# Another order of the same operations, and the buffers that follow from it, in a linear-attention and MoE kernel

## The chip, the core and the metric

One Trainium2 chip, one core. The metric is the time of one launch in device microseconds (us): the median of three runs, with the lowest and highest beside it.

## The reference

Eight batches of eight heads, 576 tokens each, head width 64. A feature map is applied to q and k, a linear attention follows, and its output, as 4608 tokens of width 512, goes through a block with an inner width of 1024. All in float32.

```python
def phi(x):
    proj = np.einsum('bhsd,df->bhsf', x, w_phi)            # 128 features
    proj = proj - np.max(np.abs(proj), axis=-1, keepdims=True)
    return np.concatenate([np.exp(proj), np.exp(-proj)], axis=-1)
q_p, k_p = (phi(q), phi(k))
kv = np.einsum('bhsf,bhsd->bhfd', k_p, v)
z = np.sum(k_p, axis=2)
num = np.einsum('bhsf,bhfd->bhsd', q_p, kv)
den = np.einsum('bhsf,bhf->bhs', q_p, z)[..., None] + 1e-06
# x = num / den, heads side by side: 4608 x 512
h = x @ w_in
sm = softmax(h)
solu = h * sm
ln = (solu - mean(solu)) / np.sqrt(var(solu) + 1e-06) * g_ln
out = ln @ w_out
```

## The kernel before

**Units and tiles.** The attention is cut into 16 units, two to a batch. A unit has two halves, each a pair of heads; the text writes "unit 5, half 1". The second part has 36 tiles of 128 tokens, nine to a pair of batches. One engine queue works on both at once: matmuls of the tiles stand between those of the units.

**One half of a unit.** Keys come in by `k_load` (rawk) and values by `v_load` and `v_half_load` (rawv, vz). TensorE (PE) projects the keys (pjk); VectorE (DVE) takes the largest absolute value of each row (m) and subtracts it (dk); ScalarE (ACT) makes the two exponentials (ek); GpSimd (POOL) sums them over tokens (zt, zacc). Then `visit` does three things without a break on PE: the numerators of the half before (num), the sum of keys times values of this half (kvT), and the denominators of the half before (den). The numerators read kvf, which is kvT turned by way of DRAM: DVE turns blocks (kvs), SyncE (SP) writes them out (dk), and four transfers read them back (kvf). So each visit needs the four reads that follow the visit before. Units 0 to 2 are handled apart: their query features are projected and turned on PE (pjq, dq, dT, fq); units 0 and 1 turn kvT on PE (kvt). Later units use q as loaded twice (rawq), split in two fp32r parts on POOL (hq), projected (pq) and turned on DVE (blk). The denominators are inverted on DVE (dE, cmr), written to DRAM (d) and read back spread over 64 partitions by two transfers (rb); POOL then multiplies (`divide`, xa and xb).

**One tile.** `moe_hi` and `moe_lo` split the input in two fp32r parts (mxh, mxl), `moe_h` multiplies with w_in in two halves of 12 matmuls (h), DVE takes the maximum (nm), ACT the exponential (eu), DVE the product, DVE turns blocks (ub), SP writes them (du) and four transfers read them back (uTs), ACT and POOL split them (uhs, uls), and `moe_o` multiplies with w_out in two halves of 12 matmuls (o). ACT scales the result (os) and SP stores it (out). The last three tiles turn on PE instead (uh, ul).

**Weights.** w_in and w_out arrive as 64-bit floats in eight transfers of 1024 KB (`w_load`, wraw; parts 0 to 3 are w_in, parts 4 to 7 w_out) and are rebuilt as float32: one pass on ACT and three on DVE for each part (`w_rebias`, `w_bits`), then the w_in parts are split (win_h on ACT, win_l on POOL), and the w_out parts are scaled, centred on DVE (`w_center`, eight passes w<-w,cms) and split (w_out_h, w_out_l). The first tile's h needs all four win_l and the division of both units of batch 0.

**What sets the order.** Each operation is registered with `op`, with the operations that it follows and the buffers that it takes. `Plan.order` (line 232) then walks through a table of 2621 operation numbers, `SEQUENCE` (line 50): it checks that what an operation follows stands ahead of it, and gives each new tile the buffer of its kind that was freed first.

```python
        for i in SEQUENCE:
            o = self.ops[i]
            assert written.issuperset(o["after"]), o["name"]
            written.add(o["name"])
            for tag, t in o["alloc"]:
                slot[t] = free[tag].pop(0)
```

`InOrder` (line 255) keeps every instruction in program order. So each engine, and SP's queue of transfers, runs its operations in the order of the table, and an instruction that waits holds up all that stand behind it on its engine. All 595 transfers are issued by SP. All work is recorded in a helper, so nearly every row of the profile has line 263.

Of the kernel before, what the change touches and what calls it, by code (L numbers as in the profile page):

```python
# [50 lines left out]
    88, 99, 0, 3, 2, 136, 126, 132, 102, 7, 89, 90, 100, 103, 198, 104, 199, 127, 107, 95, 108, 91, 101, 96,  # L51
    130, 8, 131, 14, 92, 133, 230, 105, 128, 97, 186, 137, 197, 134, 93, 129, 35, 98, 145, 224, 135, 94, 142,
    138, 106, 148, 9, 109, 149, 143, 139, 144, 118, 140, 234, 146, 150, 41, 10, 15, 187, 114, 11, 141, 151, 119,
    110, 164, 147, 165, 16, 120, 188, 121, 115, 153, 111, 152, 200, 205, 17, 112, 53, 231, 166, 154, 116, 201,
    36, 193, 232, 189, 156, 4, 233, 117, 167, 202, 155, 194, 169, 113, 37, 203, 225, 18, 158, 168, 157, 122,
    204, 190, 195, 28, 295, 38, 196, 6, 42, 226, 39, 12, 191, 228, 13, 170, 192, 235, 227, 171, 229, 172, 240,
    123, 159, 173, 241, 243, 236, 160, 216, 245, 47, 43, 54, 238, 44, 244, 174, 242, 175, 161, 55, 29, 296, 45,
    162, 246, 217, 328, 124, 30, 247, 249, 284, 248, 207, 56, 251, 250, 125, 218, 40, 208, 176, 31, 219, 48,
    209, 32, 177, 178, 179, 210, 49, 163, 252, 180, 212, 46, 237, 213, 254, 50, 214, 253, 255, 215, 51, 211,
    329, 256, 239, 436, 297, 206, 21, 386, 52, 303, 332, 304, 271, 57, 397, 262, 268, 285, 263, 59, 286, 269,  # L60
    333, 60, 58, 220, 633, 437, 330, 291, 273, 61, 264, 287, 270, 22, 331, 292, 272, 298, 221, 257, 438, 293,
    62, 299, 258, 288, 294, 387, 300, 289, 181, 344, 63, 265, 5, 182, 222, 23, 301, 305, 290, 259, 67, 302, 260,
    76, 314, 338, 79, 183, 73, 334, 184, 85, 64, 261, 306, 315, 310, 316, 398, 307, 311, 24, 317, 223, 267, 345,
    266, 346, 68, 19, 33, 65, 274, 20, 308, 275, 276, 309, 34, 335, 278, 277, 347, 279, 439, 349, 339, 348, 336,
    280, 312, 440, 318, 337, 388, 185, 313, 340, 319, 25, 350, 320, 321, 66, 351, 281, 74, 282, 389, 26, 341,
    352, 390, 75, 393, 391, 353, 27, 394, 441, 355, 442, 354, 372, 342, 373, 356, 77, 322, 374, 283, 70, 323,
    468, 358, 366, 1871, 357, 82, 367, 359, 324, 368, 343, 445, 360, 375, 1913, 1872, 443, 69, 395, 1873, 444,
    86, 361, 80, 1914, 446, 362, 377, 447, 550, 469, 614, 81, 405, 392, 1874, 399, 376, 406, 87, 396, 325, 83,
    326, 470, 363, 400, 1875, 448, 327, 369, 401, 511, 1876, 449, 416, 402, 407, 370, 1877, 371, 471, 408, 78,
    1915, 412, 450, 413, 417, 409, 472, 1880, 451, 477, 452, 473, 403, 475, 84, 404, 1916, 474, 410, 1881, 476,  # L70
    501, 551, 418, 478, 479, 453, 422, 1917, 1882, 500, 1883, 378, 552, 853, 1918, 1884, 1885, 379, 512, 1919,
    1892, 364, 411, 71, 1893, 419, 480, 380, 1894, 1886, 1922, 1923, 481, 423, 454, 424, 414, 482, 457, 455, 72,
    381, 458, 555, 553, 483, 1887, 1924, 425, 1895, 554, 484, 459, 1878, 1925, 415, 426, 456, 427, 556, 428,
    1920, 420, 559, 1926, 557, 1888, 1927, 558, 1896, 421, 560, 1897, 365, 429, 1928, 1898, 485, 460, 1901, 461,
    1934, 561, 1929, 486, 582, 1902, 583, 430, 1935, 502, 1903, 462, 382, 463, 520, 1930, 489, 584, 431, 503,
    664, 1904, 507, 519, 504, 505, 1921, 514, 432, 562, 506, 1936, 513, 563, 508, 490, 383, 564, 515, 509, 530,
    433, 516, 491, 1905, 517, 434, 565, 585, 435, 566, 587, 487, 567, 586, 1937, 464, 588, 488, 384, 510, 1906,
    518, 531, 568, 589, 1938, 591, 1931, 696, 590, 532, 1939, 571, 592, 665, 1879, 1940, 536, 572, 385, 1943,
    1932, 593, 1944, 666, 492, 573, 493, 1907, 1945, 1908, 1946, 521, 1947, 494, 697, 1948, 465, 594, 1889, 595,
    569, 615, 522, 596, 570, 698, 526, 523, 537, 524, 667, 538, 525, 597, 1909, 668, 626, 1949, 495, 1933, 533,  # L80
    975, 527, 1890, 625, 528, 466, 529, 496, 1950, 699, 539, 598, 671, 700, 1910, 540, 541, 542, 534, 497, 669,
    627, 673, 670, 498, 1951, 672, 535, 674, 1899, 467, 675, 543, 499, 1941, 574, 1955, 1956, 2018, 599, 1957,
    576, 575, 600, 603, 544, 676, 545, 1958, 677, 577, 778, 678, 2019, 546, 679, 740, 616, 1959, 680, 729, 681,
    547, 628, 617, 1960, 548, 1952, 618, 549, 604, 1961, 619, 620, 621, 601, 644, 622, 2020, 629, 623, 630, 624,
    1964, 1976, 645, 602, 1965, 703, 605, 701, 578, 705, 631, 2021, 810, 682, 632, 646, 702, 704, 706, 1900,
    650, 2022, 1942, 685, 2023, 779, 2024, 606, 683, 2027, 1966, 1967, 1968, 579, 1969, 580, 728, 607, 707,
# [1182 lines left out]
```

## Time and profile before

| what | value |
|---|---|
| median of 3 runs | 719.25 us (719.08 to 719.99) |
| the profiled execution | 717.91 us |
| its span, first to last instruction | 716.1 us |
| granted TensorE clock, mean | 0.997 |
| PE busy | 694.4 us (97%) |
| DVE, ACT, POOL busy | 483.5 (68%), 368.7 (51%), 513.7 us (72%) |
| moved by DMA | 109.96 MB, mean 154 GB/s |

The profiled execution is 1.34 us shorter than the median of the timed runs; 1.8 us of it lie outside the span. A row of the timeline gives the start and the length in us, the engine, the operation, the tiles that are written and read, the shapes and the count, and in brackets the idle time before it with what ended that. Rows of neighbouring like operations are merged. SPq is SP issuing a transfer, not the transfer itself.

### The profile page before, as it was taken

To read this page: it belongs to the slowest core of one execution; us is meant where nothing else is said; L and a number is where in the kernel's file an instruction comes from. 1 tells how busy PE (TensorE), PEld (TensorE's weight loads), DVE (VectorE), ACT (ScalarE), POOL (GpSimd) and SP (SyncE) were. 2 spreads that over 40 slices of the span, in tenths; PEclk is the share of its full clock that TensorE was granted. 3 is DMA by queue.
4 is the path that set the end of the run, shared out by engine and by line. 5 is a ranking of instruction groups with operands and counts; after the bars stand their busy time and mean duration, and the time that the engine had idled before them with its cause. 6 is when DMAs were issued, how large, how long until landed. Compare 5 with 4: busy or idle time off the path is not lost.

```text
span 716.1 us, 13369 instructions
## 1 busy us (share of the span) xinstructions
PE 694.4 (97%) x4858; PEld 517.8 (72%) x4858; DVE 483.5 (68%) x795; ACT 368.7 (51%) x683; POOL 513.7 (72%) x501
## 2 busy tenths in 40 slices
PE   6999889999999999999999999999999999999997
PEld 5656567777777777777776777777787777788886
DVE  5999878656867678478566688676687574544422
ACT  4888645644753555546555555545544554324221
POOL 1136999996889878887978987986877777445151
PEclk9999999999999999999999999999999999999999
DMA  7784365644763565637357367745664443512331
GB/s 258 286 274 103 79 181 167 189 136 118 199 189 121 159 194 159 199 106 205 111 161 183 118 179 185 192 133 139 177 182 119 144 135 77 155 56 72 125 102 75
DMA packets 113649, 109.96 MB, mean 154 GB/s; under 512 B 57648, under 2 KB 90928, under 8 KB 113072
## 3 DMA queue, kind: packets, MB, share of 16 engines
q1 hardware_dynamic: 113584, 109.11, 52.7%
q8 instruction: 39, 0.64, 0.4%
q14 instruction: 26, 0.21, 0.1%
HBM read 76.68 MB, written 32.39 MB: 152 GB/s over the span
## 4 chain that ended last, share of the span: by engine, by line
PE 81%; DVE 6%; DMA 5%; SPq 2%; ACT 2%; issue 2%; POOL 2%; POOLq 0%; ACTq 0%
PE o L263 26%; PE h L263 24%; PE kvT L263 9%; PE num L263 8%; PE pjk L263 5%; PE den L263 4%; PE pq L263 3%; DVE w L263 2%; SPq L263 2%; DMA kvf<-dk 2%; DVE m L263 1%; DMA dk<-kvs 1%; POOL xa L263 1%; DMA rawk<-in_k 1%; DMA rb<-d 1%
## 5 line engine op out<-in xcount | busy, mean ns | idle before, releaser
L263 ACT ACTIVATE ek<-dk 128x512 f32<-128x512 f32 (+1 forms) x160 | 86.5, 584 | 50.7 <-DVE dk L263 49.0
L263 PE MATMUL o<-w_out_h,uhs 128*128 128x512 f32 x264 | 106.5, 403 | 0.0
L263 PE MATMUL o<-w_out_h,uls 128*128 128x512 f32 x264 | 104.2, 395 | 0.0
L263 PE MATMUL o<-w_out_l,uhs 128*128 128x512 f32 x264 | 104.1, 394 | 0.0
L263 POOL TENSOR_TENSOR uls<-uTs,uhs 128x1024 fp32r<-128x1024 f32 x33 | 79.1, 2396 | 27.6 <-ACT uhs L263 21.1
L263 PE MATMUL h<-win_h,mxh 128*128 128x512 f32 x288 | 93.1, 404 | 0.1
L263 PE MATMUL h<-win_l,mxh 128*128 128x512 f32 x288 | 89.4, 392 | 0.0
L263 PE MATMUL h<-win_h,mxl 128*128 128x512 f32 x288 | 89.4, 391 | 0.0
L263 DVE TENSOR_REDUCE nm<-h 128x1 f32<-128x1024 f32 x36 | 43.8, 1217 | 60.1 <-PE h L263 60.0
L263 POOL TENSOR_TENSOR zt<-ek 128x512 f32<-128x512 f32 x52 | 67.2, 1293 | 16.8 <-ACT ek L263 15.2
L263 POOL TENSOR_TENSOR hq<-rawq,hq 64x1152 fp32r<-64x1152 f32 x26 | 69.0, 2655 | 9.6 <-issue 6.1
L263 PE MATMUL num<-fq,kvf 128*64 128x288 f32 x512 | 69.2, 412 | 2.9 <-DMA kvf<-dk 2.1
L263 ACT ACTIVATE fq<-pT 128x576 f32<-128x576 f32 x104 | 68.1, 678 | 7.4 <-DVE pT L263 7.4
L263 ACT ACTIVATE eu<-h,nm 128x1024 f32<-128x1024 f32 x36 | 40.1, 1115 | 53.2 <-DVE nm L263 47.6
L263 PEld LDWEIGHTS h<-win_l,mxh 128*128 128x128 f32 x288 | 54.0, 188 | 12.1
L263 PEld LDWEIGHTS h<-win_h,mxl 128*128 128x128 f32 x288 | 54.1, 188 | 12.1
L263 DVE TENSOR_TENSOR eu<-h,eu 128x1024 f32<-128x1024 f32 x36 | 43.8, 1217 | 27.4 <-ACT eu L263 27.3
L263 PE MATMUL kvT<-ek,rawv 128*64 128x256 f32 x512 | 61.1, 380 | 0.0
L263 DVE TENSOR_REDUCE m<-pjk 128x4 f32<-128x512 f32 (+1 forms) x80 | 48.4, 621 | 18.3 <-PE pjk L263 18.2
L263 DVE STREAM_TRANSPOSE blk<-pq 128x288 f32<-128x288 f32 x104 | 45.4, 457 | 22.0 <-PE pq L263 17.8
L263 PEld LDWEIGHTS h<-win_h,mxh 128*128 128x128 f32 x288 | 50.8, 189 | 10.9 <-issue 1.4
L263 PEld LDWEIGHTS num<-fq,kvf 128*64 128x64 f32 x512 | 34.5, 136 | 32.7 <-issue 10.2
(107 smaller groups left out, 1444.4 us busy)
## 6 DMA issues: line engine op xcount, KB each, us to landing
du<-ub SPq DMA_DIRECT2D x33, 512.0 KB, 2.8
uTs<-du SPq DMA_DIRECT2D x132, 128.0 KB, 3.4
rawq<-in_q SPq DMA_DIRECT2D x26, 576.0 KB, 4.5
rb<-d SPq DMA_DIRECT2D x64, 144.0 KB, 3.6
out<-os SPq DMA_DIRECT2D x36, 256.0 KB, 3.1
rawk<-in_k SPq DMA_DIRECT2D x32, 256.0 KB, 3.8
rawv<-in_v SPq DMA_DIRECT2D x32, 256.0 KB, 4.0
dk<-kvs SPq DMA_DIRECT2D x28, 192.0 KB, 2.3
```

Of the source, the lines that this page charges most:

```text
L263: return self.tc.keep_in_program_order(method(*args, **kwargs))
```

## The change

Only the table `SEQUENCE` changes; nothing else in the file does. The same 2621 operations stand in another order, so each engine gets the same instructions in another order, and tiles get other buffers of their kind. The order was searched on replays of the kernel that hold the transfer times measured in a run. The table's first line, as an instance (its other lines are changed in the same way):

```diff
 SEQUENCE = (
-    88, 99, 0, 3, 2, 136, 126, 132, 102, 7, 89, 90, 100, 103, 198, 104, 199, 127, 107, 95, 108, 91, 101, 96,
...
+    99, 2, 0, 3, 88, 126, 132, 7, 14, 102, 4, 136, 35, 103, 90, 5, 104, 105, 106, 127, 107, 95, 89, 91, 100, 96,
...
 )
```

How far operations move differs by engine. Of PE's 436 operations none moves by more than 11 places among those of PE, and the mean is 1.2 places; POOL's mean is 2.0, DVE's 2.8, ACT's 3.4; SP's 595 transfers move by 6.4 on average and up to 74. Three places follow.

**SP, the first loads.** This is what SP issues from the first weight part on, before the change. wraw0, wraw1 and wraw4 are weight parts of 1024 KB; rawk_144 is the last key block of unit 0 (its third), rawv and vz are values.

```order
L263 DMA wraw0_114<-in_w_in 128x2048
L263 DMA rawv_116<-in_v 128x512
L263 DMA vz0_74<-in_v 64x128
L263 DMA vz1_76<-in_v 64x128 x2
L263 DMA rawk_144<-in_k 128x512
L263 DMA rawv_148<-in_v 128x512
L263 DMA vz0_74<-in_v 64x128
L263 DMA wraw1_160<-in_w_in 128x2048
```

And the same stretch after it, where rawk_149 is that key block, rawv_153 and the vz the values that unit 0's first visit reads:

```order
L263 DMA wraw0_110<-in_w_in 128x2048
L263 DMA wraw1_112<-in_w_in 128x2048
L263 DMA rawq2_118<-in_q2 128x512
L263 DMA wraw4_120<-in_w_out 128x2x1024
L263 DMA rawk_149<-in_k 128x512
L263 DMA rawv_153<-in_v 128x512
L263 DMA vz0_74<-in_v 64x128 x2
L263 DMA rawv_174<-in_v 128x512
```

Two more weight parts and a query block now stand ahead of the key block and the values. In front of these rows the small loads have moved too: the two halves of w_phi (wph) now come ahead of unit 0's first large key block.

**POOL, up to the first tile.** Before the change, from the split of unit 3's queries (hq) on; the xa are the last three of the four divisions of batch 0 (unit 1 half 0, unit 0 half 1, unit 1 half 1), the win_l the last three w_in parts, mxl the input of tile 0:

```order
L263 TENSOR_TENSOR hq_769<-rawq_682,hq_769 64x1152
L263 TENSOR_TENSOR xa_628<-E_650,rb_850 128x576
L263 TENSOR_TENSOR win_l_99<-w32_1_298,win_h_98 128x1024
L263 TENSOR_TENSOR win_l_99<-w32_3_561,win_h_98 128x1024
L263 TENSOR_TENSOR xa_628<-E_621,rb_890 128x576
L263 TENSOR_TENSOR w_out_l_1043<-w32_4_380,w_out_h_922 128x512
L263 TENSOR_TENSOR w_out_l_1043<-w32_5_531,w_out_h_922 128x512
L263 TENSOR_TENSOR win_l_99<-w32_2_835,win_h_98 128x1024
L263 TENSOR_TENSOR xa_628<-E_949,rb_1047 128x576
L263 TENSOR_TENSOR mxl_1143<-xa_628,mxh_1112 128x512
```

After it:

```order
L263 TENSOR_TENSOR hq_672<-rawq_462,hq_672 64x1152
L263 TENSOR_TENSOR win_l_99<-w32_3_537,win_h_98 128x1024
L263 TENSOR_TENSOR xa_637<-E_693,rb_781 128x576
L263 TENSOR_TENSOR w_out_l_942<-w32_4_335,w_out_h_916 128x512
L263 TENSOR_TENSOR win_l_99<-w32_1_220,win_h_98 128x1024
L263 TENSOR_TENSOR xa_637<-E_624,rb_903 128x576
L263 TENSOR_TENSOR win_l_99<-w32_2_887,win_h_98 128x1024
L263 TENSOR_TENSOR w_out_l_942<-w32_4_335,w_out_h_916 128x512
L263 TENSOR_TENSOR xa_637<-E_944,rb_1044 128x576
L263 TENSOR_TENSOR mxl_1157<-xa_637,mxh_1098 128x512
```

The win_l of weight part 3 now stands ahead of the first of these divisions; the other rows between that division and mxl are of the same kinds, with the two w_out_l apart instead of together. On SP, the transfers that feed this division (rb of unit 1 half 0) stood behind the denominators of unit 0 half 1 (d); now they stand ahead of them. On DVE, two of the eight centring passes (w<-w,cms) have moved from a run of six to a place some 25 operations later, behind the passes of unit 2's last query block. A key block of unit 3 (rawk, its third) that SP issued behind the denominators of unit 2 half 0 is now issued five transfers ahead of them.

**SP, between a write and its four reads.** Before the change, from the turned kvT of unit 5 half 1 (dk) to the last of the four reads (kvf) that the first visit of unit 6 needs; uTs, out, rb, rawv and rawq belong to other work:

```order
L263 DMA dk_2540<-kvs_2538 128x384
L263 DMA rawv_2554<-in_v 128x512
L263 DMA rawq_2559<-in_q 128x1152
L263 DMA kvf_2581<-dk_2540 32x12x32
L263 DMA uTs_2530<-du_2515 32x4x256
L263 DMA out_0<-os_2321 128x512
L263 DMA kvf_2581<-dk_2540 32x12x32
L263 DMA rb_2522<-d1_2448 64x2x288
L263 DMA rawv_2613<-in_v 128x512
L263 DMA kvf_2581<-dk_2540 32x12x32
L263 DMA uTs_2530<-du_2515 32x4x256 x2
L263 DMA kvf_2581<-dk_2540 32x12x32
```

After it:

```order
L263 DMA dk_2542<-kvs_2540 128x384
L263 DMA kvf_2544<-dk_2542 32x12x32
L263 DMA rawq_2546<-in_q 128x1152
L263 DMA uTs_2598<-du_2538 32x4x256
L263 DMA out_0<-os_2384 128x512
L263 DMA kvf_2544<-dk_2542 32x12x32 x2
L263 DMA d1_2647<-cmr_2640 128x9
L263 DMA kvf_2544<-dk_2542 32x12x32
```

Eight other transfers stood between the write and the last read, and now four. For the next visit (unit 6 half 0 to half 1) there were seven, and now four. For other visits the number rises or falls: from 6 to 9 after unit 4 half 0, from 0 to 4 after unit 5 half 0, from 4 to 7 after unit 7 half 0, from 12 to 7 after unit 11 half 1, from 4 to 9 after unit 12 half 1. The PE work between one visit and the next stays the same for all but four of the visits from unit 3 on.

In the tail, where only tiles are left, the o of tile 23 moves 11 places forward on PE; between its last h and its first o stand seven halves of other tiles, where there were 13 and four sets of transposes. The last matmuls of the program are the same two halves of o in either order, of tiles 27 and 33, in exchanged places.

270 rows, old and new, of the table SEQUENCE are left out of this document.

## The prediction

> **What bounds the kernel now.** First the page's busy times and the busy time by stretch (columns: PE, PEld, DVE, ACT, POOL, the granted clock, DMA share, GB/s).
>
> ```profile
> PE 694.4 (97%) x4858; PEld 517.8 (72%) x4858; DVE 483.5 (68%) x795; ACT 368.7 (51%) x683; POOL 513.7 (72%) x501
> ```
>
> ```profile
> 0.00:20.00 20.00, 13.22 (x137) 10.50 (x137) 12.82 (x22) 7.91 (x14) 2.26 (x17) 0.91 0.81 272
> 20.00:40.00 20.00, 19.69 (x249) 13.65 (x243) 19.33 (x30) 18.65 (x42) 2.69 (x1) 1.00 0.73 253
> 40.00:60.00 20.00, 17.36 (x193) 10.54 (x190) 19.18 (x27) 17.26 (x36) 12.54 (x5) 1.00 0.70 229
> 60.00:85.00 25.00, 21.94 (x266) 14.30 (x265) 23.93 (x34) 16.86 (x39) 17.80 (x10) 1.00 0.42 109
> 85.00:120.00 35.00, 32.45 (x209) 24.80 (x209) 27.25 (x44) 19.66 (x38) 33.88 (x28) 1.00 0.58 159
> 120.00:380.00 260.00, 258.30 (x1804) 192.58 (x1804) 180.67 (x315) 139.89 (x254) 219.46 (x208) 1.00 0.57 160
> 380.00:640.00 260.00, 259.17 (x1704) 192.73 (x1697) 170.09 (x289) 126.26 (x230) 201.38 (x200) 1.00 0.52 145
> 640.00:716.10 76.10, 72.30 (x326) 58.74 (x324) 30.21 (x39) 22.18 (x36) 23.69 (x36) 0.99 0.29 94
> ```
>
> The reader is to see two regimes. From 120 us on PE is the bound: of the 520 us to 640 it is idle 1.7 + 0.8 = 2.5 us, and in the last stretch 3.8 us, nearly all after its last matmul, where the last tile is scaled and stored. An order can't remove PE's work, so behind 120 us there are 2.5 us to win and any amount to lose. Before 120 us PE is idle 6.8 + 0.3 + 2.6 + 3.1 + 2.6 = 15.4 us. There from 20 to 85 us DVE is the bound (62.4 of 65 us busy): it rebuilds the weights beside the first units, and PE gets its work from it. Next the waits of PE, in the first 120 us and then from 120 to 700 us:
>
> ```profile
> PE pjk L263 <- DMA wph<-in_w_phi: 4.6, 1, 4.6
> PE pjk L263 <- DMA rawk<-in_k: 2.1, 1, 2.1
> ```
>
> ```profile
> PE num L263 <- DMA kvf<-dk: 1.7, 2, 1.0
> ```
>
> 4.6 us are the first load and stay within some tenths. So at most some 13 us of the whole can be had (10.8 ahead of 120 us, 2.5 behind), and what moves at the start counts only as far as the order gets DVE through its work sooner.
>
> **The change part by part.** The sum is made against the profiled execution, 717.91 us (span 716.1), and carried to the median, which is 1.34 higher.
>
> *(a) The first loads.* Three rows on transfers issued in the first 9 us (count, KB, median time from issue to landing):
>
> ```profile
> wraw<-in_w_in SPq DMA_DIRECT2D x1, 1024.0 KB, 7.3
> vz<-in_v SPq DMA_DIRECT2D x3, 32.0 KB, 7.0
> wph<-in_w_phi SPq DMA_DIRECT2D x2, 32.0 KB, 2.4
> ```
>
> A transfer of 32 KB took 2.4 us ahead of the 1024 KB weight part and 7.0 us behind it: transfers of SP's queue land in turn. In the new order three weight parts stand ahead of unit 0's last key block. Up to and with this block SP has issued 64 + 2 x 32 + 256 + 256 + 64 + 1024 + 1024 + 256 + 1024 + 256 = 4288 KB, 4.39 MB. At the 272 GB/s of the first stretch they have landed after 16.1 us; a few tenths of the first loads' delay come on top, so I take 17. Then come its projection and DVE's first pass over it, today here (and the first kvT matmul, which also needs values that now land later):
>
> ```profile
> 15.51 1.16 PE L263 MATMUL pjk<-wph,rawk 64*128 64x128 f32 x16
> 16.60 1.95 PE L263 MATMUL kvT<-ek,rawv 128*64 128x256 f32 x16
> ```
>
> ```profile
> 17.47 0.68 DVE L263 TENSOR_REDUCE m<-pjk 128x4 f32<-128x512 f32 x1
> ```
>
> 17 + 1.16 = 18.2 us in place of 17.47, 0.7 late. DVE can't fill the time: in the new order this pass stands ahead of three others (two over the query block, about 0.6 each start to start, and the weight pass of 1.1) that are done before it today, and two short ones have been done instead (0.6 and 0.2). That is 1.5 more, so DVE is behind by 0.7 + 1.5 = 2.2 us. Part of it is given back, since the data for the next passes are then there: DVE's waits from 20 to 60 us are
>
> ```profile
> DVE dk L263 <- ACT ek L263: 1.3, 2, 0.7
> ```
>
> So I take +1.0 (2.2 - 1.3, rounded up), from 0 if it lands by 15 us to +2.5 if none is given back.
>
> A rule of the Trainium skill would price this otherwise. "DMA: Bandwidth & Descriptors", section "Queues, rings and completion order", says that completion is not FIFO per issuing engine, as a later transfer may finish its write first. By that alone the key block, issued about 3 us sooner than today, would not be late at all, and this term would be nothing. The rows of 7.0 and 2.4 us speak against reading it so here; the same section also has each ring take descriptors in order.
>
> *(b) The divisions ahead of the first tile.* The chain of waits runs through POOL here. SP and the landing of its two d, then POOL:
>
> ```profile
> 57.71 0.33 SPq L263 DMA_DIRECT2D d<-cmr  x1
> 60.63 0.33 SPq L263 DMA_DIRECT2D d<-cmr  x1
> 61.05 1.28 SPq L263 DMA_DIRECT2D rb<-d  x2
> ```
>
> ```profile
> d<-cmr SPq DMA_DIRECT2D x2, 4.5 KB, 1.4
> ```
>
> ```profile
> 67.09 1.42 POOL L263 TENSOR_TENSOR xa<-E,rb 128x576 f32<-128x576 f32 x1 [6.47 <-DMA rb<-d]
> 68.46 5.69 POOL L263 TENSOR_TENSOR win_l<-w,win_h 128x1024 fp32r<-128x1024 f32 x2
> 81.28 1.85 POOL L263 TENSOR_TENSOR xa<-E,rb 128x576 f32<-128x576 f32 x1
> 83.86 1.27 POOL L263 TENSOR_TENSOR mxl<-xa,mxh 128x512 fp32r<-128x512 f32 x1 [0.73 <-ACT mxh L263]
> ```
>
> The denominators of unit 1 half 0 went out at 57.71, but SP stood before the next d until 60.63, and the two rb came behind it. In the new order they come ahead: up to 61.05 - (57.71 + 1.4) = 1.9 us sooner. And a win_l of about 2.4 us moves into POOL's 6.47 us of idleness. Together POOL could reach mxl 1.9 + 2.4 = 4.3 us sooner. What is late next is DVE: unit 1's last denominators and the last weight passes gate the last division and the last win_l, and they stand only two or three places earlier, by the two centring passes that have left the place ahead of them: 2 x 0.6 = 1.2 us of DVE work. DVE's own times here:
>
> ```profile
> 61.29 3.69 DVE L263 TENSOR_TENSOR w<-w,cms 128x512 f32<-128x512 f32 x6
> 79.74 3.95 DVE L263 TENSOR_TENSOR w<-w,cms 128x512 f32<-128x512 f32 x2
> 85.62 0.48 DVE L263 STREAM_TRANSPOSE blk<-pq 128x288 f32<-128x288 f32 x1 [1.34 <-PE pq L263]
> 91.11 1.22 DVE L263 TENSOR_REDUCE nm<-h 128x1 f32<-128x1024 f32 x1 [2.41 <-PE h L263]
> 92.78 0.41 DVE L263 TENSOR_TENSOR dk<-pjk,m 128x256 f32<-128x256 f32 x1
> ```
>
> A centring pass costs 0.6 us while POOL rests and 2.0 while POOL works. Two of the cheap ones move behind 84 us, where POOL works: 2 x 1.4 = 2.8 us dearer, in front of nm. What hides them is DVE's idleness there, 1.34 + 2.41 = 3.75 us; a first tile that comes 2 us sooner takes most of that cover away. I take -2.0 for (b): the 1.2 of DVE work moved back and about 0.8 from POOL and PE; from -4.3 (POOL alone counts) to 0 (DVE alone).
>
> *(c) Unit 3's last key block.*
>
> ```profile
> 94.07 1.16 PE pjk L263 x16
> ```
>
> ```profile
> 87.00 0.32 SPq L263 DMA_DIRECT2D d<-cmr  x1
> 87.92 0.91 SPq L263 DMA_DIRECT2D rawk<-in_k  x2
> ```
>
> This block is the second of the pair at 87.92, held behind the d at 87.00, and PE waits 2.1 us for it (the rawk row above), until its projection begins at 94.07. Now it is issued ahead of d. But DVE's passes up to 92.78 + 0.41 = 93.2 free the banks that it writes, so of the 2.1 us only some 0.9 can go: -0.5 (-0.9 to 0), on top of (b).
>
> *(d) The four reads of kvf.* The two waits of 1.7 us are those of unit 6's two visits. Eight and seven other transfers stood between write and last read, now four and four. An issue costs SP about 0.64 us (the rb row: 1.28 for two), so the last read goes out some 2.5 and 1.9 us sooner, more than either wait. -1.5 (-1.7 to 0).
>
> *(e) Where the new order has less room.* Other visits have three to five more transfers in that place, 2 to 3 us each. For most the PE work between two visits covers it, as their waits today are too short to be listed. In the tail, tile 23 now has seven halves between its h and its o:
>
> ```profile
> 144.41 2.80 PE o L263 x12
> ```
>
> 7 x 2.8 = 19.6 us, against its way through DRAM:
>
> ```profile
> L263 DVE TENSOR_REDUCE nm<-h 128x1 f32<-128x1024 f32 x36 | 43.8, 1217 | 60.1 <-PE h L263 60.0
> L263 POOL TENSOR_TENSOR uls<-uTs,uhs 128x1024 fp32r<-128x1024 f32 x33 | 79.1, 2396 | 27.6 <-ACT uhs L263 21.1
> du<-ub SPq DMA_DIRECT2D x33, 512.0 KB, 2.8
> uTs<-du SPq DMA_DIRECT2D x132, 128.0 KB, 3.4
> ```
>
> Five passes of about 1.2 us (nm, two for eu, ub, uhs), 2.8, four issues of 0.5, 3.4 and 2.4: 16.6 us, so it holds if nothing is in its way. I take +0.6 for all of (e), from 0 to +2.5 (four visits at 0.6).
>
> Sum: +1.0 - 2.0 - 0.5 - 1.5 + 0.6 = -2.4 us: 715.5 in a profiled execution like this one, 719.25 - 2.4 = 716.9 in the median.
>
> **The rivals.** *A: the early weights cost nothing.* Small loads don't wait for the weight parts, (a) turns into a gain of the 1.3 us that DVE waits for data, and the sum is -1.3 - 2.0 - 0.5 - 1.5 + 0.6 = -4.7: 714.5. For it speaks that the weight passes are DVE's largest load; against it the 32 KB at 7.0 us. This is the outcome of the skill's rule on completion in (a). 0.18. *B: DVE stays behind.* The key block and the values land late, nothing is given back by 60 us, and the dearer centring passes come on top, so that DVE reaches nm later than today. (a) is +2.5, (b) 0, (c) 0, (d) -1.5 and (e) +0.6: +1.6, 720.9. It decides from a lag of 2 us at 60 us, where (a) eats (b). For it speaks that DVE is 96% busy there and can't catch up. 0.18. *C: what is won at the start is given back.* PE comes sooner to visits that wait for the same chains of transfers, other visits get new waits, and (d) alone is left against (e) at its middle: about 719. For it speaks that only 2.5 us are idle behind 120 us, while dozens of chains were moved. 0.19. The forecast has the rest, 0.45.
>
> **How the numbers follow.** The time is the forecast's, 716.9. Its own bounds are about -4 to -0.8. With A below and B above, the range that leaves out 2 in 10 is 713.4 to 720.9. A run can tell about 0.2% from no change, 1.4 us. Faster by more: A whole and nine tenths of the forecast, 0.18 + 0.40 = 0.58. Same: C but for a little, and the rest of the forecast, 0.24. Slower: B and that little of C, 0.18.
>
> **What would show it.** Right, if unit 0's first kvT matmul comes later than 16.60 us while tile 0's first h comes one to two us sooner, POOL's wait of 6.47 us is cut below 4, and the waits for kvf of unit 6 are gone. (a) is wrong if DVE takes up unit 0's last key block by 16 us. (b) is wrong if h doesn't come sooner though POOL does. (e) is wrong if the idle time of PE from 120 to 640 us rises over 2.5 us. The whole is wrong if PE is through its first 120 us of work no sooner than today.

## The result, and the profile after

The changed kernel takes 729.3 us (median of 4 runs, 727.17 to 729.97) against 719.41 us for the kernel before (4 runs, 719.08 to 719.99): a ratio of 1.0136, with a 95% interval of 1.0116 to 1.0157. It is slower by about 10 us where 2.4 us less were forecast, and outside the range. The profiled execution is 729.56 us, 11.65 more than that of before. Among the runs of the experiments below two were slow, one of e1 (1972.5 us) and one of the kernel before beside it (868.7 us); the ratios leave them out, and e1's median without it is 725.9 us.

The stretches of the changed kernel, with the columns of the first table by stretch (PE, PEld, DVE, ACT, POOL, the granted clock, DMA share, GB/s):

```profile
0.00:20.00 20.00, 9.83 (x71) 8.05 (x71) 8.84 (x17) 6.90 (x11) 2.27 (x17) 0.78 0.81 288
20.00:40.00 20.00, 20.00 (x235) 13.82 (x232) 18.30 (x28) 16.06 (x35) 0.00 (x0) 0.88 0.78 262
40.00:60.00 20.00, 16.61 (x184) 10.55 (x184) 17.29 (x21) 14.58 (x31) 7.65 (x4) 0.91 0.50 159
...
120.00:380.00 260.00, 258.10 (x1777) 192.22 (x1776) 179.87 (x314) 138.02 (x249) 220.16 (x210) 1.00 0.57 162
380.00:640.00 260.00, 255.28 (x1714) 190.70 (x1713) 173.38 (x293) 129.03 (x234) 200.23 (x191) 1.00 0.53 149
```

Two losses are to be seen. In the first 60 us DVE, the engine that bounds that stage, does 8.84 + 18.30 + 17.29 = 44.4 us of work, against 12.82 + 19.33 + 19.18 = 51.3 before: 6.9 us less. And from 120 to 640 us PE is idle 1.9 + 4.7 = 6.6 us, against 2.5.

The same is read operation by operation. In the following, the lag is the start of a matmul in one profiled execution minus the start of the same matmul in that of before. For the changed kernel it is +7.8 us at the mean of the weights (PE's cm, 57.96 before), +5.3 at tile 0's first h, +6.9 at unit 3's second visit (118 us), +6.2 at unit 7's first visit (259 us), +8.0 at unit 8's first (298 us) and +11.6 at 632 us and at the end. So 7 us are lost at the start, 0.8 is won by 259 us, and over 5 are lost behind it. These are single executions; how far two of them lie apart with the same instructions is said under the table of the experiments.

The waits of PE in the changed kernel, in the first 120 us and then from 120 to 700 us:

```profile
PE pjk L263 <- DMA rawk<-in_k: 4.1, 3, 2.4
...
PE pq L263 <- POOL hq L263: 1.9, 1, 1.9
```

```profile
PE num L263 <- DVE eu L263: 1.7, 1, 1.7
PE num L263 <- DMA kvf<-dk: 1.6, 2, 1.1
PE pq L263 <- DVE dk L263: 1.4, 1, 1.4
PE num L263 <- DVE mv L263: 1.3, 1, 1.3
```

Keys are waited for three times instead of once, and a wait for POOL's split of unit 3's queries (hq) is new. In the 4 us behind that wait, from 99.5 to 103.5 us, the granted clock was 0.57, which is 0.43 x 4 = 1.7 us more. Behind 120 us the two waits for kvf at unit 6 are gone; the four longest stand at unit 7's second visit (283 us), ahead of unit 11's queries (392 us), at unit 11's second visit (440 us) and at unit 15's first (594 us).

The longest wait for keys, as PE's row, and the SP rows that lead to it. In the SP rows the rawk at 40.68 is unit 1's last key block, which was issued at 22.86 before:

```profile
48.54 1.86 PE L263 MATMUL pjk<-wph,rawk 64*128 64x128 f32 x14 [2.42 <-DMA rawk<-in_k]
```

```profile
28.78 0.33 SPq L263 DMA_DIRECT2D wraw<-in_w_in  x1
...
30.16 0.71 SPq L263 DMA_DIRECT2D wraw<-in_w_out  x1
37.10 0.33 SPq L263 DMA_DIRECT2D d<-cmr  x1
...
38.48 0.38 SPq L263 DMA_DIRECT2D wraw<-in_w_in  x1
...
40.68 0.60 SPq L263 DMA_DIRECT2D rawk<-in_k  x1
```

What SP itself waited for from 20 to 45 us:

```profile
SPq L263 <- DVE cmr L263: 6.1, 1, 6.1
SPq L263 <- DVE w L263: 5.2, 1, 5.2
```

The new order put this block behind four weight parts (three are shown) and behind the write of unit 0's denominators (d<-cmr). SP stood 5.2 us for a weight buffer that DVE frees, then 6.1 us for DVE to make those denominators, and the block landed at 48.49 us, 7.8 us after its issue, behind the 1024 KB issued at 38.48.

### The profile page after: what moved, and what is told of

It is laid out like the page before. It is cut to its first block, busy times and chain, and to the rows that moved or that the text cites. A ratio compares the mean times of both kernels' runs of the same rounds, so it can differ in the third digit from the quotient of the medians.

```text
span 727.8 us, 13359 instructions
## 1 busy us (share of the span) xinstructions
PE 700.1 (96%) x4858; PEld 523.5 (72%) x4858; DVE 482.6 (66%) x795; ACT 370.9 (51%) x683; POOL 513.6 (71%) x501
## 4 chain that ended last, share of the span: by engine, by line
PE 83%; DMA 8%; POOL 2%; DVE 2%; SPq 2%; issue 1%; ACT 1%; POOLq 0%; DVEq 0%; ACTq 0%
PE o L263 25%; PE h L263 23%; PE kvT L263 10%; PE num L263 8%; PE pjk L263 6%; PE den L263 4%; PE pq L263 3%; DMA rawk<-in_k 3%; SPq L263 2%; DMA kvf<-dk 1%; DMA du<-ub 1%; PE dT L263 1%; DMA dk<-kvs 1%; POOL hq L263 1%; DMA rawq<-in_q 1%
## 5 line engine op out<-in xcount | busy, mean ns | idle before, releaser
L263 ACT ACTIVATE fq<-pT 128x576 f32<-128x576 f32 x104 | 68.0, 677 | 16.7 <-DVE pT L263 16.7
L263 PE MATMUL kvT<-ek,rawv 128*64 128x256 f32 x512 | 62.6, 387 | 0.0
L263 PE MATMUL pjk<-wph,rawk 64*128 64x128 f32 (+1 forms) x544 | 51.2, 309 | 8.0 <-DMA rawk<-in_k 4.1
```

Source lines behind the costliest of these rows:

```text
L263: return self.tc.keep_in_program_order(method(*args, **kwargs))
```

## The experiments

Sixteen kernels ran, of fourteen orders: e15 is e3's and e16 is e5's again. Each differs from before or from the changed kernel only in `SEQUENCE`. In the edits, BEFORE and AFTER are the two tables, and a table's SP operations are written as numbers: 107 is unit 0's last key block, 89, 100, 101 and 108 its values, 205 unit 1's last key block, 14, 21, 28, 35 and 53 the weight parts 1, 2, 3, 4 and 7, 160 unit 0's denominators, 161 and 162 their broadcasts. The tables are printed with fewer lines, so what has line 263 in the kernel before has line 259 in these. All results (median, ratio to the runs of before on the same chip with its 95% interval, and the lag of the profiled execution in us; the ratio is an estimate of its own and isn't exactly the quotient of two medians):

| kernel | median us | ratio | lag at 118 us | at 298 us | at 632 us |
|---|---|---|---|---|---|
| changed | 729.3 | 1.0136 [1.0116, 1.0157] | +6.9 | +8.0 | +11.6 |
| e1 before, new loads | 726.4 | 1.0069 [1.004, 1.0098] | +7.3 | +6.4 | +6.4 |
| e9 e1, unit 1's block early | 725.6 | 1.0099 [1.0067, 1.0131] | +5.4 | +5.6 | +5.6 |
| e10 before, unit 1's block late | 723.8 | 1.0068 [1.0045, 1.0092] | +4.2 | +4.7 | +5.1 |
| e2 changed, old loads | 734.8 | 1.0199 [1.0169, 1.0229] | +10.4 | +14.9 | +17.4 |
| e3 changed, unit 1's block early | 722.5 | 1.0031 [1.0011, 1.0051] | +1.0 | +4.3 | +5.8 |
| e15 as e3 | 723.1 | 1.0058 [1.0036, 1.008] | +0.2 | +1.7 | +4.8 |
| e4 old start, new rest | 726.2 | 1.0086 [1.0052, 1.012] | +0.9 | +4.4 | +6.1 |
| e13 changed, unit 7's reads ahead | 725.4 | 1.0091 [1.0068, 1.0114] | +4.2 | +3.8 | +7.7 |
| e5 e3, unit 7's reads ahead | 721.4 | 1.0028 [1.0005, 1.0052] | +1.3 | +0.3 | +2.4 |
| e16 as e5 | 721.1 | 1.0037 [1.0018, 1.0057] | +1.0 | +1.0 | +2.9 |
| e7 e3, a weight part later | 722.2 | 1.0055 [1.0029, 1.0081] | +0.4 | +3.6 | +7.1 |
| e14 all three places | 718.5 | 0.9997 [0.9976, 1.0017] | -2.1 | -3.2 | -0.3 |
| e6 unit 6 alone new | 725.9 | 1.0107 [1.0075, 1.014] | +0.9 | +8.1 | +9.1 |
| e8 e7 up to unit 7 | 716.5 | 0.9978 [0.9957, 0.9999] | -0.5 | +1.1 | +0.8 |
| e11 up to unit 8 | 720.9 | 1.001 [0.999, 1.003] | -0.7 | -1.7 | +3.4 |
| e12 up to unit 9 | 717.9 | 0.9981 [0.9964, 0.9998] | +0.3 | -0.3 | +2.0 |

The profiled execution of before is 717.91 us and the medians of its runs beside these kernels lie between 718.7 and 720.4, so the lags are about one to two us larger than the medians tell; and a kernel's own profiled execution can lie 3 us from its median (e7: 725.2 against 722.2). e4 and e6 have the start of before, operation for operation, and still show +2.5 and +2.6 us at the mean of the weights, where two passes of DVE ahead of it took 4.6 us together instead of 2.5, and +0.9 at 118 us. e13 has the start of the changed kernel and shows +4.2 at 118 us instead of +6.9; e7, e8, e11, e12 and e14 share one start and lie between -2.1 and +0.4. So a lag can't be read closer than one to three us, and the sizes below are taken from medians where there are medians for them.

### Which loads: e1, e9, e10, e2, e3

e1 gives the kernel before SP's first 29 transfers in the new order:

```diff
-SP: ... 7, 89, 100, 198, 199, 107, 108, 101, 14, ... 35, ... 205, 53, 28, ...
+SP: ... 7, 14, 136, 35, 107, 89, 100, 101, 108, ... 28, 206, 199, 53, 205, ...
```

> The kernel before, with one thing of the change: SP's first 29 transfers in the new order; every other engine keeps its order. Theory (SP's transfers land in the order of issue, and the weight parts put ahead of unit 0's last key block and unit 1's hold up PE and DVE): first kvT matmul at 20 to 22 us instead of 16.60, PE about 5 to 7 us behind by unit 1, end at 724 to 727 us. Rival (the loss at the start comes from the new order of the passes on DVE and ACT, and the loads alone are nearly free, as the prediction's term (a) had it): 719 to 721 us.

Measured: +7.3 us at 118 us and +6.4 at the end; the first kvT matmul at 20.14 us. The loads alone cost what the theory said, and the orders of the other engines need not be touched for that. Moving one transfer alone, 205, in the kernel before (e10):

```diff
-SP: 205, 53, 28, 295, 6, 160, 47, 161, 296, 162
+SP: 53, 28, 295, 6, 160, 47, 161, 205, 296, 162
```

> The kernel before with one transfer moved: unit 1's last key block is issued behind unit 0's first denominator broadcast, seven places later, as in the new order. Theory (this one place holds up PE and with it DVE): the block lands at 43 to 46 us instead of 26.8, PE stands for it 2 to 4 us at its projection, 3 to 6 us behind at 125 us and at the end, ratio 1.004 to 1.008. Rival (it holds only together with the late first block; alone the room behind 40 us takes it): under 1.5 us at the end.

PE's row, and DVE's share by stretch:

```profile
45.23 1.01 PE L259 MATMUL pjk<-wph,rawk 64*128 64x128 f32 x6 [5.08 <-DMA rawk<-in_k]
```

```profile
20.00:40.00 20.00, 19.64 (x260) 13.61 (x249) 19.60 (x31) 18.29 (x41) 2.72 (x1) 1.00 0.66 227
40.00:60.00 20.00, 14.57 (x138) 9.24 (x138) 14.61 (x18) 12.37 (x27) 6.52 (x3) 0.83 0.69 226
```

The block landed at 45.19 us instead of 26.79, and PE stood 5.08 us for it, longer than the 2 to 4 expected. DVE, which has 19.18 us of work from 40 to 60 us before, has 14.61. That is a steady loss: +4.2 at 118 us, +5.1 at the end, a ratio of 1.0068. One transfer, seven places later, makes half of what the whole change lost (by medians 723.76 against 718.73). Now the other way round, the changed kernel with 205 put back in front of weight part 3 (e3):

```diff
-SP: 28, 206, 199, 53, 160, 436, 285, 21, 334, 295, 161, 205, 162
+SP: 205, 28, 206, 199, 53, 160, 436, 285, 21, 334, 295, 161, 162
```

> The changed kernel with a single transfer moved: unit 1's last key block is issued ahead of the fourth weight part (the 29th place of before) instead of eleven places later. Theory A (two hold-ups of about equal weight, unit 0's block landing at 18.1 us and unit 1's at 48.5 us): kp of unit 1 starts some 8 us sooner, 2 to 3 us come back at the end, 726 to 727.5. Theory B (the first hold-up sets DVE's whole schedule, the second only fills a wait that is there anyway): within 1 us of 729.3.

It came back by more than theory A said: +1.0 instead of +6.9 us at 118 us, and 722.5 us. DVE is full again from 20 us on, in e3's stretches:

```profile
0.00:20.00 20.00, 10.40 (x73) 8.75 (x74) 8.99 (x18) 6.91 (x11) 2.26 (x17) 0.80 0.82 300
20.00:40.00 20.00, 20.00 (x243) 13.91 (x243) 19.41 (x29) 17.54 (x37) 0.00 (x0) 0.94 0.84 277
40.00:60.00 20.00, 18.79 (x244) 12.34 (x244) 19.82 (x28) 18.37 (x41) 13.08 (x5) 1.00 0.45 146
```

8.99 + 19.41 + 19.82 = 48.2 us of DVE work by 60 us, 3.1 less than before, and the lag at cm is 3.1. The first 20 us cost 3.8 of DVE work, 0.7 of it is made up by 60 us, and most of the rest by 118 us. Theory B fell, and theory A's price was too low. e9 does to e1 what e3 does to the changed kernel:

```diff
-SP of e1: 28, 206, 199, 53, 205
+SP of e9: 205, 28, 206, 199, 53
```

> The kernel of e1 (before, with SP's first 29 transfers in the new order) with unit 1's last key block put back ahead of the fourth weight part, as in e3. What is left of the change is what the prediction's term (a) spoke of: weight parts ahead of unit 0's last key block and values. Theory (that block's delay is a small cost, the other block the large one): 1 to 3 us behind before at 125 us and to the end, 720 to 722.5 us, ratio 1.001 to 1.004. Rival (the first hold-up carries the cost by itself, 3.5 us at unit 1 and not made up): 5 to 6.5 us, 724 us or more.

Here the theory fell: e9 stays at +5.4 us, hardly better than e1, though the block lands at 29.89 us instead of 42.19. With the weight parts ahead of unit 0's block and the other engines in the old order, the first hold-up costs about 5 us by itself and covers the second. With the other engines in the new order the same first hold-up is made up by 118 us (e3). Which engine's order does it was not tried: e3 and e9 differ on PE, DVE, ACT and POOL and in SP's later transfers. So the loads and the rest of the new order belong together, and e2 shows it from the other side. It is the changed kernel with SP's first 29 transfers as before:

```diff
-SP: ... 7, 14, 136, 35, 107, 89, 100, 101, 108, ... 28, 206, 199, 53, ...
+SP: ... 7, 89, 100, 198, 199, 107, 108, 101, 14, ... 35, ... 205, 53, 28, ...
```

> The changed kernel with SP's first 29 transfers put back into the order of before; all else stays changed. Theory (the loads' order): 5 to 7 us come back, 722 to 724 us, and what is left over 719.4 are the new waits after 240 us. Rival (order on DVE and ACT): under 2 us come back, over 727 us.

Neither theory holds; it is slower than the changed kernel (734.8 us). ACT's row shows one reason why it begins badly:

```profile
16.62 1.10 ACT L259 ACTIVATE wraw<-wraw 128x1024 f32<-128x1024 f32 x1 [6.25 <-DMA wraw<-in_w_in]
```

In the new order ACT takes weight part 1 ahead of the exponentials of unit 0. With the old loads that part lands at 16.60, and ACT stands 6.25 us in front of work that it could do. The same kernel stands another 7.9 us for a part of w_out.

### Unit 7's visit: e4, e5, e13, e15, e16

e4 has the kernel before's order up to unit 4's first visit:

```diff
-SEQUENCE = AFTER
+SEQUENCE = BEFORE[:605] + [i for i in AFTER if i not in BEFORE[:605]]
```

> Everything up to unit 4's first visit (about 125 us) in the order of before, everything behind it in the new order. Theory (the new waits after 240 us belong to the new order itself: 1.9 at unit 7, 0.7 to 1.4 each at units 10, 11 and 15, against 1.1 won at unit 6): 721 to 723.5 us. Rival (those waits arise only because the start is late, as the changed chains then meet other transfers): 717 to 719 us, that is the gain of (d) is all that is left.

At 726.2 us it is slower than both expectations. The new order's later part loses 5.2 us by itself (+0.9 to +6.1), so it isn't the late start that makes those waits. The largest is at unit 7's second visit, which needs the four reads that follow the first (the expectations below name the first, after which these reads stand). In three fences, e3's SP rows ahead of it, its PE row, and two stretches of 4 us around it:

```profile
265.38 0.44 SPq L259 DMA_DIRECT2D du<-ub  x1
...
266.88 0.74 SPq L259 DMA_DIRECT2D kvf<-dk  x1
271.14 0.33 SPq L259 DMA_DIRECT2D uTs<-du  x1
271.52 0.58 SPq L259 DMA_DIRECT2D kvf<-dk  x1
...
273.75 1.23 SPq L259 DMA_DIRECT2D kvf<-dk  x2
```

```profile
277.65 2.94 PE L259 MATMUL num<-fq,kvf 128*64 128x288 f32 x14 [2.12 <-DMA kvf<-dk]
```

```profile
274.00:278.00 4.00, 1.88 (x11) 1.22 (x11) 3.93 (x5) 0.69 (x3) 3.60 (x8) 1.00 0.90 202
278.00:282.00 4.00, 4.00 (x24) 2.69 (x22) 2.07 (x5) 2.75 (x4) 2.67 (x2) 0.57 0.47 180
```

The first read of tile 12 (uTs at 271.14) stands between the first and the second read of kvf. It needs tile 12's write (du at 265.38) to have landed, which took 5.7 us; SP stood for that, and the three reads that PE needs stood behind it although their data had been ready since 266.4. PE waited 2.12 us, and the granted clock was 0.57 in the 4 us behind it, which is 0.43 x 4 = 1.7 us more: the lag grows from 0.35 to 4.29. e5 is e3 with those reads in front (881 to 884 are the reads of kvf, 2134 to 2137 those of tile 12, 976 values of unit 8):

```diff
-SP: 881, 2134, 882, 2135, 2136, 976, 883, 884, 2137
+SP: 881, 882, 883, 884, 2134, 2135, 2136, 976, 2137
```

> The changed kernel with unit 1's last key block early (the order of e3_key_block_early) and, at unit 7's first visit, the last three reads of kvf put ahead of tile 12's first three reads and a load of values, so that SP doesn't stand for tile 12's write (from 266.9 to 271.1 us in e3) in front of them. Theory (one blocked read in front of the others makes PE's wait of 2.1 us at 277.7, and the granted clock of 0.57 in the 4 us behind it costs as much again): the wait is gone, the clock stays at 1.00, unit 8's first visit comes 3 to 4 us sooner, 718.5 to 719.5 us. Rival (the number of transfers between write and read is what counts, the DVE passes are late next, as in the changed kernel, where the row names DVE eu): under 1.5 us come back, 721 to 723 us.

SP's rows in e5, at the same place:

```profile
266.77 2.86 SPq L259 DMA_DIRECT2D kvf<-dk  x4
271.19 1.28 SPq L259 DMA_DIRECT2D uTs<-du  x3
```

The wait is gone and the lag at unit 8 is 0.3, as the theory had it; but the median is only 1.1 us below e3's, taken at another time beside other runs of before. So both were run again side by side:

> The kernel of e3 again, beside e5's on the same chip in the same rounds. Theory (unit 7's wait and the low clock behind it cost 3 to 4 us in most runs): the median is 2.5 to 4 us over that of e5. Rival (the wait is so long only in the profiled run; in most runs it is short and the clock stays): under 1.5 us over that of e5, as the first two medians had it, 722.5 and 721.4.

> The kernel of e5 again, beside e3's in the same rounds. Theory: 2.5 to 4 us under e3's median, 718.5 to 720 us. Rival: under 1.5 us below it, 721 us or more.

723.12 against 721.09, 2.0 us, between the two expectations, with ratio intervals that overlap. e15's profile shows one reason why it can be less than the theory's: the same wait in its PE row, and no low clock in the 4 us behind it:

```profile
276.78 2.16 PE L259 MATMUL num<-fq,kvf 128*64 128x288 f32 x16 [2.28 <-DMA kvf<-dk]
```

```profile
278.00:282.00 4.00, 4.00 (x48) 2.70 (x48) 1.52 (x5) 3.28 (x5) 2.83 (x2) 1.00 0.22 83
```

The wait costs its 2.1 to 2.4 us in e3, e4, e7 and e15, and 3.4 in e2, where SP stands in front of the same read (issued at 280.76 us, the one before it at 276.34); the 1.7 us on top came in four of these five profiles, all but e15's. e13 makes e5's edit in the changed kernel alone:

> The changed kernel with the second of the three places alone: unit 7's last three reads of kvf ahead of tile 12's first three reads and of a load of values, unit 1's key block left late. Theory (in the changed kernel the wait of 1.7 us at 283.05 us comes from the same stand of SP, and what DVE is late with comes at about the same time): 1 to 2 us come back, 727.3 to 728.5 us. Rival (the row names DVE eu, so SP's stand isn't the last to end there): nothing comes back, within 0.5 us of 729.3 and the wait still at unit 7.

The wait at unit 7 is gone (lag +3.8 at both 259 and 298 us), so SP's stand was its cause, though the row named DVE (num <- DVE eu). The whole came out lower than the theory said, 725.4. The start cost 4.2 us here and 6.9 in the changed kernel's profile, with the same instructions; about half of that difference is the wait for hq, 1.52 us here without a low clock behind it, 1.94 there with one.

### Weight part 4 behind unit 0's block: e7, e14

e7 is e3 with weight part 4 moved behind unit 0's last key block and values:

```diff
-SP: 7, 14, 136, 35, 107, 89, 100, 101, 108
+SP: 7, 14, 136, 107, 89, 100, 101, 108, 35
```

> The changed kernel with unit 1's last key block early and the third weight part (1 MB) issued behind unit 0's last key block and values instead of ahead of them. Theory (the key block lands some 2.7 us sooner, about 14.7, and what the new order wins up to the first tile, as in the prediction's term (b), is then kept): kp of unit 0's last block at 15 us, tile 0's first h at 83 to 85 us, 719.5 to 721.5 us. Rival (DVE and ACT stand in the new order for other data, so that an earlier block changes nothing at 85 us): tile 0's first h within 0.5 us of the 85.9 us of e3, 722 to 723 us.

The block's projection in e3 and in e7:

```profile
17.55 2.16 PE L259 MATMUL pjk<-wph,rawk 64*128 64x128 f32 x16 [1.35 <-DMA rawk<-in_k]
```

```profile
16.66 1.95 PE L259 MATMUL pjk<-wph,rawk 64*128 64x128 f32 x16
```

The block, issued within 0.1 us of the same time, lands at 15.37 instead of 17.42 us, and tile 0's first h comes at 84.11 us: 1.3 us ahead of before, in e3 0.5 behind. But 1.2 of these 1.8 us are lost by 118 us: behind the wait for hq, 1.95 us here, the granted clock was 0.60 from 94 to 98 us (0.4 x 4 = 1.6 us), while in e3 it stayed at 1.00 behind a wait of 1.90. Nothing is left in the median (722.2 against 722.5, taken at different times); the low clock at unit 7 came here too. e14 has e7's and e5's edits together, three places in SP's order and nothing else against the changed kernel:

> The changed kernel with the three places of SP's order put right (unit 1's key block early, the third weight part behind unit 0's block, unit 7's reads ahead); no other engine's order differs from the changed kernel. Theory (the three gains add up): 718.5 to 720.5 us, ratio 0.999 to 1.002, what is left over being the waits at units 10, 11 and 15. Rival (they don't add up, since those later waits take up what the start wins): as e7, 721.5 us or more.

718.49 us, a ratio of 0.9997 (0.9976 to 1.0017): the loss is gone. Its stretches and PE's waits from 120 us on:

```profile
0.00:20.00 20.00, 11.72 (x89) 9.48 (x91) 10.82 (x21) 8.14 (x15) 2.27 (x17) 0.83 0.82 305
20.00:40.00 20.00, 19.24 (x275) 13.42 (x271) 19.88 (x30) 18.54 (x37) 2.14 (x1) 1.00 0.95 322
40.00:60.00 20.00, 18.77 (x205) 11.86 (x202) 19.72 (x29) 18.31 (x40) 13.12 (x6) 1.00 0.42 124
...
380.00:640.00 260.00, 256.75 (x1672) 193.76 (x1673) 166.27 (x284) 127.13 (x229) 198.47 (x195) 1.00 0.51 146
```

```profile
PE pq L259 <- DVE dk L259: 1.4, 1, 1.4
PE num L259 <- DMA kvf<-dk: 1.0, 1, 1.0
PE num L259 <- DVE mv L259: 1.0, 1, 1.0
PE num L259 <- issue: 0.6, 1, 0.6
```

DVE does 50.4 us of work by 60 us. In this profile PE waits 1.5 us for hq with no low clock behind it, and is 2.1 us ahead at 118 us and 3.2 at unit 8; from 380 to 640 us it is idle 3.2 us where before it was 0.8, and the lead is spent.

From the four kernels that ran side by side, each place by a difference of medians: unit 1's block 725.43 - 721.09 = 4.3 (e13, e16), the reads at unit 7 723.12 - 721.09 = 2.0 (e15, e16), weight part 4 721.09 - 718.49 = 2.6 (e16, e14). Together 8.9, and 718.5 + 8.9 = 727.4 lies at the lower end of the changed kernel's runs (727.17 to 729.97, median 729.3). The last two are small against the spread of the runs, and for the weight part e3 and e7 gave only 0.3, by their ratios even a loss (1.0031 and 1.0055). That the three places together make the loss is shown by e14; their single sizes are known to one or two us.

### Parts of the new order in the old: e6, e8, e11, e12

e6 has the new order from unit 5's second to unit 7's first visit alone. In this kernel and in the next three the operations stand in each engine's order as the edit says; between engines they are merged so that each tile finds a buffer.

```diff
-SEQUENCE = BEFORE
+SEQUENCE = BEFORE[:838] + (AFTER up to 1081) + (the rest in the order of BEFORE)
```

> The order of before up to unit 5's second visit (198 us), the new order from there to unit 7's first visit (259 us), the order of before again behind it. It holds term (d) alone. Theory ((d) is real and keeps to itself): PE is 1.0 to 1.3 us sooner at unit 7's first visit and stays so to the end, ratio 0.9978 to 0.999. Rival (given back behind it): the ratio is 1 within 0.001 and the lag at the end is 0.

Neither: where the two orders are joined a wait of its own arises, 3.48 us in front of unit 6's first visit, and the kernel ends 9.1 us behind. It says nothing on (d). e8, e11 and e12 are e7 (e11 and e12 with e5's edit) up to unit 7's first, unit 8's second and unit 9's first visit, and the order of before behind that:

```diff
-SEQUENCE = AFTER
+SEQUENCE = (e7's table up to 1081) + (the rest in the order of BEFORE)
```

> The kernel of e7 up to unit 7's first visit (259 us), the order of before behind it. Theory (what is lost behind 260 us belongs to the new order there): PE has no wait behind 260 us that before hasn't, the end is 5 to 6 us sooner than in e7, 714.5 to 717.5 us, a ratio of 0.993 to 0.997. Rival (before's later order fits only its own times, and a unit 7 that comes sooner meets transfers that aren't there): 718 us or more, ratio 0.998 or more.

> The kernel of e7 with unit 7's reads ahead as in e5, up to unit 8's second visit (317 us), the order of before behind it. Theory (wins at the start, (d), and no new wait later): PE is level with before or up to 1 us ahead at 317 us and at the end, 714.5 to 717 us, ratio 0.994 to 0.998, no slower than e8. Rival (the seam between the two orders costs a wait of its own, as at 221 us in e6): a wait of over 1 us behind 317 us, ratio 0.999 or more.

> As e11, with the seam to the order of before at unit 9's first visit (339 us) instead of unit 8's second (317 us). Theory (the wait of 1.7 us at 334.8 us in e11 and its low clock are the seam's own, and e11 was 1.7 us ahead in front of it): no wait there, PE about 1.7 us ahead of before from 317 us to the end, 715.5 to 717.5 us, ratio 0.995 to 0.998. Rival (every seam costs its own wait, or the lead is lost where before's order waits for transfers that the clock sets): level or behind at the end, ratio 0.999 or more.

e8 reaches 716.5 us, 0.9978 (0.9957 to 0.9999), e12 717.9, 0.9981 (0.9964 to 0.9998): by the median and by the interval both are faster than the kernel before, if by little, and both are faster than the changed one. They aren't told apart. e8 is 5.7 us faster than e7, as its theory had it, though its ratio lies between the two expectations. The gain isn't seen in their profiles, which end 0.8 and 2.0 us behind that of before, so where it lies is not shown; e12's is not ahead at unit 8 (-0.3), as its theory had it, and has the low clock behind the wait for hq (0.60 from 94 to 98 us). In e11 the rival came: it is 1.7 us ahead at unit 8, and then the seam costs a wait and a low clock, its row and stretch:

```profile
334.77 0.79 PE L259 MATMUL o<-w_out_h,uls 128*128 128x512 f32 x1 [1.70 <-POOL uls L259]
```

```profile
334.00:338.00 4.00, 3.23 (x8) 2.56 (x9) 4.00 (x6) 2.65 (x6) 3.84 (x4) 0.57 0.45 131
```

e12 has none there, but one of 1.41 us at 350 us. So a seam between two orders can bring waits that neither has; that the seam makes these two was read from their place and not tried.

## Why the prediction was wrong

**(a) is the step that failed.** "Up to and with this block SP has issued ... 4.39 MB": the queue was counted up to unit 0's last key block and no further. The estimate for that block was near (17 us, landed at 18.09, though issued 1.0 us sooner than before and not 3), and the lag that followed from it larger than the 2.2 us taken: DVE's pass came 3.0 us late, and the first kvT matmul 5.2, since the values landed at 18.9 to 19.8 us and PE's projection ran 2.2 us instead of 1.16, at a granted clock of 0.50 (18.2 to 20.4 us) where before it was 1.00 (15.5 to 16.7 us). The two rows in the changed kernel:

```profile
18.23 2.17 PE L263 MATMUL pjk<-wph,rawk 64*128 64x128 f32 x16 [1.34 <-DMA rawk<-in_k]
```

```profile
20.43 0.69 DVE L263 TENSOR_REDUCE m<-pjk 128x4 f32<-128x512 f32 x1 [1.81 <-PE pjk L263]
```

What was not looked at is the other key block that the same lines move: unit 1's went from the 25th to the 37th place of SP, past four weight parts and past a write that waits for DVE. The place of that one transfer is 4.3 us of the loss by medians, 6.0 by the profiles of the changed kernel and e3, 3.2 by those of e13 and e16. The term was taken as +1.0 with a bound of +2.5; by medians the two places are 4.3 + 2.6 = 6.9 us, and the profiles show +6.9 at 118 us in the changed kernel and +4.2 in e13. Of the bound, "none is given back" was right for before's order of the other engines and wrong for the new one: e9 keeps about 5 us of the first hold-up, e3 makes it up.

**Rival A** didn't happen. In each of the 18 profiles here all 595 transfers land in the order in which SP issued them, and moving 1024 KB behind unit 0's block (e7) brought the block 2.05 us sooner with the same time of issue. The rule of the Trainium skill ("DMA: Bandwidth & Descriptors", section "Queues, rings and completion order"), that completion is not FIFO per issuing engine, may hold for other mixes of transfers; no run here shows it. It says what isn't guaranteed; that a small load would overtake large ones was the prediction's reading of it.

**Rival B** had the mechanism: DVE behind at 60 us and not caught up. It set the point at 2 us, and the lag there was 7.8. Its price of +2.5 for (a) was too small, as (a)'s was, and so its time of 720.9 was too low by 8 us.

**(b)** was right, if seen apart from the start. POOL's wait of 6.47 us is 3.94 in the changed kernel and in e14:

```profile
71.82 2.39 POOL L263 TENSOR_TENSOR win_l<-w,win_h 128x1024 fp32r<-128x1024 f32 x1 [3.94 <-ACT win_h L263]
```

Between cm and tile 0's first h the lag falls by 2.4 us in the changed kernel, 2.6 in e3 and e7 and 3.1 in e14, while kernels with before's order on DVE and POOL lose 0.6 to 1.1 of theirs on the same way (e10, e4, e1). That leaves about 2, as forecast, though by lags alone; in e14, where the loads are in place, h comes 2.3 us ahead of before. In the changed kernel it came 5.3 late, so the test given for (b) failed for the reason of (a).

**(c)** was wrong. Unit 3's block is no longer waited for, but the projection of unit 3's next queries, which came behind the block's on PE, now stands one place ahead of it and waits for POOL: 1.9 us in the changed kernel, 1.5 in e14:

```profile
91.56 0.40 PE L259 MATMUL pq<-hq,w_hh 128*128 128x288 f32 x1 [1.52 <-POOL hq L259]
```

The prediction asked what is late next, and looked only at DVE. So instead of -0.5 the term is about nothing, and +1.7 in the executions that had the low clock behind this wait.

**(d)** came about as forecast, and is not shown by itself. The waits of unit 6's two visits are gone, and from unit 5's second visit to unit 7's first the lag falls by 1.1 us in the changed kernel and by 0.4 (e16) to 1.4 (e5, e14) in the other kernels that have the new order through this stretch, against 1.5 forecast; in e8 it rises by 0.5. With before's order there it rises by 0.3 and 0.5 in e9 and e10, but falls by 1.0 in e1, so part of it may be spread. It could not be tried alone (e6).

**(e)** was mis-sized: +0.6, up to 2.5, against 2.0 by medians for unit 7's second visit and 2.9 for the waits from unit 10 to unit 15 (e14's profile, from -3.2 to -0.3). Its own sign of being wrong came: from 120 to 640 us PE is idle 6.6 us and not 2.5. It counted the transfers between write and read. At unit 7 what decided was whether one among them waits: tile 12's read did, for a write that had just been issued. Of the later waits, those ahead of unit 11's queries and at unit 15 end with DVE passes (dk, mv) and the one at unit 11's second visit with reads of kvf; their cause was read from the rows and not tried. The tail held, as its sum had it: from 632 us to the end the lag doesn't grow.

**Rival C**, the gain given back behind 120 us, is what is left when the loads are put right: e14 wins 3.2 us by unit 8 in its profile and ends level, and its median is that of before within the interval.

In the prediction's terms, and as an estimate from medians and lags together: (a) +6.9 in place of +1.0, (b) about -2, (c) 0 to +1.7, (d) about -1, (e) +4.9 in place of +0.6, in sum 9 to 10.5 us, where 9.9 were measured. So (a) is 5.9 us of the miss of 12.3 and (e) 4.3.

## What to carry to other kernels

When an order changes, follow each transfer that moves to the work that waits for it, and not only the first one: on a queue that keeps its order, a large load put ahead, or an entry that must wait for an engine, holds up all that stands behind it, and the costliest victim here stood twenty-six entries behind the first one that was counted. Between a write and the reads that a busy engine needs, look for entries that wait, before counting entries. Two orders aren't safely cut and joined: the loads of one order belong with the work of the other engines in it (e2, e9), and three of the five joined kernels (e6, e11, e12) had a new wait of over 1 us near the place where they were joined.

## What the runs showed of the hardware

A stop of PE can cost nearly twice its length. After waits of 2.12, 2.39, 2.18 and 3.42 us at unit 7 (e3, e4, e7, e2) the granted clock was 0.57 in the next 4 us, and another 1.7 us were lost; after 2.28 us at the same place (e15) and after 1.71 us (the changed kernel) it stayed at 1.00. In e11 it was 0.57 behind a wait of 1.70 us that followed one of 0.47. The wait for hq at unit 3 shows the same with nearly equal lengths: after 1.94, 1.95 and 1.94 us (the changed kernel, e7, e12) the clock was 0.57 to 0.60 over 4 us, after 1.90 to 1.95 us (e3, e5, e8, e11, e16) it stayed at 1.00. Late loads prolong the low clock of the start as well: it was 0.50 from 11.6 to 15.0 us in before and from 11.0 to 24.7 us in the changed kernel. The Trainium skill ("TensorE: Matmul & The Clock Gate", section "HAM oscillation — how this bites in real kernels") gives idle gaps of over about 3.4 us as the ones to avoid; here shorter ones were enough, in some executions. Its section "What's actually happening" has the activity judged in a window that runs freely, which fits that the same wait is punished in one execution and not in another; in the traces' record of the clock the low stretches after waits behind 60 us last 3.41 us, and 6.83 in e6, which agrees with a fixed window; that it runs freely no run here shows.
